# An attention and two MLPs on one core: v read in runs of 2048 bytes into 72 partitions, P summed over 8 steps

## The chip, the cores and the metric

The program runs on one core of a Trainium2 chip. The metric is the device time of one execution in microseconds. A core has TensorE (PE, with its weight loads as PEld), VectorE (DVE), ScalarE (ACT), GpSimd (POOL), SyncE (SP, which here only issues DMAs), and 16 DMA engines that move the data between main memory and the 128 partitions of the on-chip buffer.

## The reference

```python
def _attn_ref(q, k, v, p):                  # q, k, v: (8, 8, 576, 64); p: (8, 8, 32, 64)
    scale = 1.0 / np.sqrt(q.shape[-1])
    def sm_attn(qq, kk, vv):
        s = scale * np.matmul(qq, kk.transpose(0, 1, 3, 2))
        s = s - np.max(s, axis=-1, keepdims=True)
        a = np.exp(s)
        a = a / (np.sum(a, axis=-1, keepdims=True) + 1e-09)
        return np.matmul(a, vv)
    p_packed = sm_attn(p, k, v)             # 32 packed rows for each head
    return sm_attn(q, p_packed, p_packed)

x = attention, as (4608, 512)
x = (silu(x @ w_gate) * (x @ w_val)) @ w_out          # d_ff 1536
out = (((x @ w1) * (x @ w2)) @ w3) @ w_out2           # d_ff 1024
```

q, k, v and p are 32-bit floats; the weights come as 64-bit floats, which the kernel reads as integers and converts itself.

## The kernel before, in words

The program has a first stage, the packed attention, and then the two MLPs, which are almost all matrix products. The change touches the first stage alone, where `p_packed` is made.

The first stage goes over 16 units u, each of 4 heads of one batch element (`b, Q = divmod(u, 2)`). For each unit, `load_kv(u, "k")` brings a tile `km` of k, 128 partitions of 18 tokens (4608 bytes in one run), and `load_kv(u, "v")` a tile `vm` of v; both are 576 KB. In `vm` a head's 576 tokens are cut into `PK` = 96 runs of `NV` = 6 tokens: partition p has, for each of 4 heads, tokens 6p to 6p+5, one run of 1536 bytes. Then:

- `pa_kT` turns k and p by products with an identity (`pk`, `pkr`) and copies them to `kT`. p lies in the tile `zp`, for all batch elements, each row twice, the second copy made on POOL by `twice_p`.
- `pa_s` forms the scores of 32 packed rows against 576 tokens for 4 heads (`psp`) and their maximum; `pa_exp` writes the exponentials to `ap`, sorted so that the tokens of one step r (token 6p+r for all p) stand together.
- `pa_T` turns `ap` step by step (`pat`, 6 transposes of 96 columns) and ScalarE copies the result to `apT`.
- `pa_P` sums over 6 steps r and 4 heads: 24 products `pP` of `apT` with `vm`, each over 96 partitions. `pa_PT` turns the result into the tile `PTd`, which all later work uses.

The order is written out by hand: a loop over steps s issues `pa_kT(s)`, `pa_s(s-1)`, `pa_PT(s-4)`, `pa_T(s-2)`, `pa_exp(s-1)`, `pa_P(s-3)`, and every engine runs its instructions in that order. Other work is hung on steps by tables: the first q tiles (`q_rows`, 4 tiles of 576 KB) and what follows from them, `raw_load` for the first weights (512 KB each: `raw_w` in rows of 1024 bytes, `raw_wo` in rows of 4096 bytes, 128 partitions), and their conversion. All loads of the stage are issued by SP, one after the other; a load whose buffer isn't free yet holds up those behind it. There are 4 buffers for k (`KVB`) and 4 for v (`VB`):

```python
            if s < U:
                pa_kT(s)
            load_kv(s - VD, "v")
            load_kv(s + KVB, "k")
```

Two loads of later stages are used in the prediction. `raw_wo` of the second MLP is read by four loads of 32 partitions each, in rows of 4096 bytes (line 329); `x2r` is read into 128 partitions in runs of 1536 bytes (line 795).

Of the kernel before, what the change touches and what calls it, by code (L numbers as in the profile page):

```python
# [8 lines left out]
F32 = mybir.dt.float32  # L9
# [6 lines left out]
ET = mybir.EngineType  # L16
M0 = None
KVB = 4
VB = 4
VD = 0  # L20
RAW0 = (7, 8, 10, 11, 12, 13, 15, 15, 15, 16.75)
WS = {10.0: (0, 0), 11.0: (0, 1), 13.25: (1, 0), 14.25: (1, 1), 15.25: (2, 0), 16.25: (2, 1)}
# [18 lines left out]
def packed_attention_moe_kernel(  # L41
# [24 lines left out]
    nc = tc.nc  # L66
    B, H, S, D = q.shape
# [3 lines left out]
    DF2 = w1.shape[1]  # L71
    HS = S // 2
    NR = S // 32
    NV = 6
    PK = S // NV
    NF = DFF // 128
    NB32 = S // 32
# [7 lines left out]
    def pool(name, side, bufs=1, **kw):  # L85
        return tc.alloc_tile_pool(name=name, bufs=bufs, side=side, reuse_waits="tile", **kw)
# [21 lines left out]
    ident = const.tile([128, 128], F32, name="ident")  # L108
# [15 lines left out]
    def psum(name):  # L124
        ps_n[0] += 1
        return ps_at[ps_n[0] % len(ps_at)].tile([128, 2, 512], F32, tag="A", name=name)

    def psum1(name):
        return psB.tile([128, 512], F32, tag="B", name=name)
# [4 lines left out]
    hs = [slice(32 * hq, 32 * hq + 32) for hq in range(4)]  # L134

    in_front, conv_rest, pin, pin_at = [True], [], {}, {}
# [338 lines left out]
    pa = pool("pa", "left", bufs=2)  # L475

    kv = {}
    zp = pa.tile([128, B, 2, 2, 64], F32, tag="zp", name="zp", bufs=1)

    def load_p(b0, b1):  # L480
        nc.sync.dma_start(zp[:, b0:b1, :, 0], p[b0:b1].rearrange("b (q h) j d -> (h j) b q d", q=2))

    def twice_p(b0, b1):
        nc.gpsimd.tensor_copy(zp[:, b0:b1, :, 1], zp[:, b0:b1, :, 0])

    def load_kv(u, nm):
        if not 0 <= u < 2 * B:
            return
        b, Q = divmod(u, 2)
        src = {"k": k, "v": v}[nm]  # L490
        if nm == "k":
            m = pa.tile([128, NR, D], F32, tag="km", name=f"km{u}", bufs=KVB)
            nc.sync.dma_start(m, src[b, 4 * Q:4 * Q + 4].rearrange("h (p r) d -> (h p) r d", r=NR))
        else:
            m = pa.tile([PK, 4, NV, D], F32, tag="vm", name=f"vm{u}", bufs=VB)
            pin_at["sp"] = nc.sync.dma_start(m, src[b, 4 * Q:4 * Q + 4].rearrange("h (p r) d -> p h r d", r=NV))
        kv[nm, u] = m
# [3 lines left out]
    def pa_kT(u):  # L501
        km = kv.pop(("k", u))

        kT = pa.tile([128, NR // 2 + 1, 128], F32, tag="kT", name=f"kT{u}")
        b, Q = divmod(u, 2)
        t1 = psum1(f"pkr{u}")
        nc.tensor.transpose(t1[:, 128:256], zp[:, b, Q].rearrange("p e d -> p (e d)"), ident)
        t = psum(f"pk{u}")
        for m in range(NR // 2):
            nc.tensor.transpose(  # L510
                t[:, m // 4, 128 * (m % 4):128 * (m % 4) + 128] if m < 8 else t1[:, 0:128],
                km[:, 2 * m:2 * m + 2, :].rearrange("p r d -> p (r d)"), ident)
        nc.scalar.copy(kT[:, 0:8], t.rearrange("p a (m n) -> p (a m) n", n=128))
        nc.scalar.copy(kT[:, 8:10], t1[:, 0:256].rearrange("p (m n) -> p m n", n=128))
        kT_t[u] = kT

    def pa_s(u):


        kT = kT_t.pop(u)  # L520
        t = psum(f"psp{u}")
        for hq in range(4):
            for e in range(2):
                es = slice(64 * e, 64 * e + 64)
                nc.tensor.matmul(
                    t[hs[hq], e, 0:HS].rearrange("j (m p g) -> j g m p", m=3, g=3), lhsT=kT[es, 9, hs[hq]],
                    rhs=kT[es, 0:9, hs[hq]].rearrange("d (g m) p -> d g m p", g=3), start=True, stop=True, tile_position=(64 * e, 32 * hq))
        mx = pa.tile([128, 1], F32, tag="mx", name=f"mx{u}")
        nc.vector.reduce_max(mx, t[:, :, 0:HS], axis=AX.XY)
        nc.vector.tensor_scalar_mul(mx, mx, -scale)  # L530
        return t, mx

    def pa_exp(u, t, mx):
        a = pa.tile([128, NV, PK], F32, tag="ap", name=f"ap{u}")
        sm = pa.tile([128, 1], F32, tag="sm", name=f"sm{u}", bufs=3)
        nc.scalar.activation(
            a.rearrange("j (m e) p -> j e m p", e=2),
            t[:, :, 0:HS].rearrange("j e (m p) -> j e m p", p=PK),
            AF.Exp, bias=mx, scale=scale, accum_out=sm)
        ap_t[u], sm_t[u] = a, sm  # L540

    def pa_T(u):
        a, sm = ap_t.pop(u), sm_t[u]
        nc.vector.tensor_scalar(sm, sm, 1e-9, None, op0=ALU.add)
        nc.vector.reciprocal(sm, sm)
        t = psum(f"pat{u}")
        for r in range(NV):
            nc.tensor.transpose(
                t[:PK, r % 2, 128 * (r // 2):128 * (r // 2) + 128],
                a[:, r], ident)  # L550
        aT = pa.tile([PK, 2, 3, 128], F32, tag="apT", name=f"apT{u}")
        pin_at["act"] = nc.scalar.copy(aT, t[:PK, :, 0:384].rearrange("p e (m n) -> p e m n", m=3))
        apT_t[u] = aT

    def pa_P(u):
        vm = kv.pop(("v", u))
        aT = apT_t.pop(u)
        sm = sm_t.pop(u)
        t = psum1(f"pP{u}")
        for r in range(NV):  # L560
            for hq in range(4):
                nc.tensor.matmul(
                    t[hs[hq], 0:64], lhsT=aT[:, r % 2, r // 2, hs[hq]], rhs=vm[:, hq, r, :],
                    start=(r == 0), stop=(r == NV - 1), tile_position=(0, 32 * hq))
        Pd = pa.tile([128, 2, 64], F32, tag="Pd", name=f"Pd{u}")
        pin_at["dve"] = nc.vector.tensor_scalar(
            Pd, t[:, 0:64].rearrange("p (o d) -> p o d", o=1).to_broadcast([128, 2, 64]), sm, None, op0=ALU.mult)
        Pd_t[u] = Pd

    def pa_PT(u):  # L570
        t = psum1(f"pPT{u}")[:, 0:128]
        nc.tensor.transpose(t, Pd_t.pop(u).rearrange("p a b -> p (a b)"), ident)
        nc.scalar.copy(PTd[:, u], t)

    U = 2 * B
    load_p(0, 1)
    load_kv(0, "k")
    load_kv(1, "k")
    load_p(1, 3)
    load_kv(2, "k")  # L580
    load_p(3, B)
    twice_p(0, 1)
    twice_p(1, 3)
    twice_p(3, B)
    for u in range(3, KVB):
        load_kv(u, "k")
    extra = {}
# [22 lines left out]
    def run(s, slot):  # L610
        for at in [at for at in extra if s + slot <= at < s + slot + 0.25]:
            for fn, args in extra.pop(at):
                fn(*args)

    last = int(max(max(extra), U + 3))
    with tc.manual_schedule(engines=M0):
        for s in range(last + 1):
            if s < U:
                pa_kT(s)
            load_kv(s - VD, "v")  # L620
            load_kv(s + KVB, "k")
            run(s, 0)
            run(s, 0.25)
            if 0 <= s - 1 < U:
                x = pa_s(s - 1)
            if 0 <= s - 4 < U:
                pa_PT(s - 4)
            run(s, 0.5)
            if 0 <= s - 2 < U:
                pa_T(s - 2)  # L630
            if 0 <= s - 1 < U:
                pa_exp(s - 1, *x)
            if 0 <= s - 3 < U:
                pa_P(s - 3)
            run(s, 0.75)
# [466 lines left out]
```

## Time and profile before

| what | value |
|---|---|
| median of 3 runs | 1412.79 us (1408.39 to 1418.39) |
| the profiled execution | 1416.25 us |
| its span, first to last instruction | 1414.5 us |
| mean granted TensorE clock over the span | 0.987 |
| PE busy, weight loads | 1358.2 us (96%), 1246.9 us (88%) |
| DVE, ACT, POOL busy | 715.7, 576.7, 401.1 us (51%, 41%, 28%) |
| bytes moved | 230.28 MB in 182471 packets, mean 163 GB/s |

Shares of busy time are means over the whole span. The stages have different limits, so the views by stretch of time say more than this table. A busy PE is not a PE at its peak, since products are pipelined.

### The profile page before, as it was taken

What the parts mean: (1) busy time and instruction counts of PE and PEld (TensorE: products, weight loads), DVE (VectorE), ACT (ScalarE), POOL (GpSimd) and SP (SyncE); (2) the same over time, 40 slices, a digit from 0 to 9 for tenths busy, and PEclk for the clock granted to TensorE, in tenths of its full rate; (3) what the DMA queues carried; (4) which work ended last, traced back from release to release, by engine and by line L of the source; (5) the groups of instructions that cost most, each with busy time, mean ns of one, the idle gap of its engine ahead of it and who ended that gap; (6) DMA issues with size and microseconds to landing.
All of it is one profiled execution on the core that took longest, in us unless ns stands there. A gap on an engine that the chain in (4) does not pass through costs nothing.

```text
span 1414.5 us, 25679 instructions
## 1 busy us (share of the span) xinstructions
PE 1358.2 (96%) x10228; PEld 1246.9 (88%) x10228; DVE 715.7 (51%) x1016; ACT 576.7 (41%) x946; POOL 401.1 (28%) x315
## 2 busy tenths in 40 slices
PE   7778989999999999999999989999999999999998
PEld 5556988999999999998988889989989899898997
DVE  2457779636585566664255467933323423334130
ACT  4576534425243353353453334623323333333231
POOL 0234233422333323254253323702202122021120
PEclk9899999999999999999999999999999999999999
DMA  9997676544345545235443236955728448175451
GB/s 257 244 217 197 185 222 210 150 152 99 116 125 169 171 101 136 61 116 153 139 132 96 67 96 243 334 192 182 235 76 253 156 154 258 58 247 178 132 159 45
DMA packets 182471, 230.28 MB, mean 163 GB/s; under 512 B 70480, under 2 KB 113488, under 8 KB 182352
## 3 DMA queue, kind: packets, MB, share of 16 engines
q1 hardware_dynamic: 182352, 228.64, 54.9%
q8 instruction: 81, 1.33, 0.4%
q14 instruction: 38, 0.31, 0.1%
HBM read 179.04 MB, written 49.55 MB: 162 GB/s over the span
## 4 chain that ended last, share of the span: by engine, by line
PE 79%; DMA 8%; DVE 5%; issue 3%; ACT 2%; POOL 1%; SPq 1%; DVEq 0%; ACTq 0%; POOLq 0%
PE px L666 19%; PE pA L975 14%; PE po L1039 14%; PE pg L454 8%; PE pv L454 8%; PE pB L975 7%; PE pC L975 4%; PE pc L422 2%; PE pw L730 2%; DMA km<-in_k_dram 1%; DMA raw_w<-in_moe_w_gate_dram 1%; DMA vm<-in_v_dram 1%; DMA raw_w<-in_moe_w_val_dram 1%; DMA raw_wo<-in_moe_w_out_dram 1%; DVE vx_w L357 1%
## 5 line engine op out<-in xcount | busy, mean ns | idle before, releaser
L90 POOL TENSOR_TENSOR ul<-u,uh 128x576 fp32r<-128x576 f32 x96 | 153.8, 1603 | 342.3 <-ACT uh L94 330.8
L995 POOL TENSOR_TENSOR c<-s,s 128x384 f32<-128x384 f32 x48 | 49.3, 1026 | 375.5 <-ACT s L990 375.4
L666 PE MATMUL px<-uh,woh 128*128 128x384 f32 x576 | 148.0, 337 | 3.0 <-DVE acc L676 2.0
L666 PE MATMUL px<-ul,woh 128*128 128x384 f32 x576 | 147.6, 336 | 2.6 <-POOL ul L90 2.6
L666 PE MATMUL px<-uh,wol 128*128 128x384 f32 x576 | 147.3, 336 | 0.0
L990 ACT COPY s<-pA 128x384 f32<-128x384 f32 x144 | 69.2, 481 | 182.9 <-PE pA L975 180.4
L463 DVE TENSOR_TENSOR u<-u,pv 128x576 f32<-128x576 f32 x96 | 71.7, 748 | 96.4 <-PE pv L454 88.9
L94 ACT CAST uh<-u 128x576 fp32r<-128x576 f32 x96 | 64.7, 674 | 134.3 <-DVE u L463 134.3
L1039 PE MATMUL po<-wo_hi,abl 128*128 128x512 f32 x288 | 112.2, 390 | 0.0
L1039 PE MATMUL po<-wo_lo,abh 128*128 128x512 f32 x288 | 112.2, 389 | 0.0
L1039 PE MATMUL po<-wo_hi,abh 128*128 128x512 f32 x288 | 112.1, 389 | 0.0
L666 PEld LDWEIGHTS px<-uh,woh 128*128 128x128 f32 x576 | 103.7, 189 | 5.7 <-DVE acc L676 2.6
L676 DVE TENSOR_TENSOR acc<-acc,px 128x768 f32<-128x768 f32 x72 | 68.1, 948 | 78.5 <-PE px L666 78.1
L666 PEld LDWEIGHTS px<-ul,woh 128*128 128x128 f32 x576 | 104.8, 189 | 3.1 <-POOL ul L90 3.1
L666 PEld LDWEIGHTS px<-uh,wol 128*128 128x128 f32 x576 | 104.9, 189 | 0.0
L90 DVE TENSOR_TENSOR abl<-ab,abh 128x768 fp32r<-128x768 f32 x48 | 48.1, 1003 | 105.4 <-ACT abh L94 105.3
L90 POOL TENSOR_TENSOR wol<-wof,woh 128x512 fp32r<-128x512 f32 x48 | 63.8, 1341 | 99.3 <-ACT woh L94 81.3
L454 PE MATMUL pg<-aTh,ch 128*128 128x288 f32 x384 | 87.9, 311 | 2.6 <-ACT u L459 2.2
L454 PE MATMUL pv<-aTh,ch 128*128 128x288 f32 x384 | 83.7, 300 | 3.4 <-ACT u L459 3.1
L459 ACT ACTIVATE u<-pg 128x576 f32<-128x576 f32 x96 | 62.4, 650 | 52.9 <-PE pg L454 51.7
L454 PE MATMUL pg<-aTh,cl 128*128 128x288 f32 x384 | 83.4, 299 | 0.0
L454 PE MATMUL pg<-aTl,ch 128*128 128x288 f32 x384 | 83.1, 298 | 0.0
(312 smaller groups left out, 3192.0 us busy)
## 6 DMA issues: line engine op xcount, KB each, us to landing
ws<-wsd SPq DMA_DIRECT2D x245, 256.0 KB, 3.1
wf<-Wd SPq DMA_DIRECT2D x36, 512.0 KB, 4.5
wsd<-ws SPq DMA_DIRECT2D x49, 256.0 KB, 3.0
km<-in_k_dram SPq DMA_DIRECT2D x16, 576.0 KB, 18.5
vm<-in_v_dram SPq DMA_DIRECT2D x16, 576.0 KB, 19.4
wof<-wod SPq DMA_DIRECT2D x36, 256.0 KB, 3.1
x2r<-X2d SPq DMA_DIRECT2D x24, 384.0 KB, 4.9
out_dram<-o SPq DMA_DIRECT2D x36, 256.0 KB, 2.0
```

The lines of the kernel that those rows point to most:

```text
L90: return eng.tensor_tensor(out=out, in0=src, in1=hi.bitcast(F32), op=ALU.subtract)
L94: nc.scalar.copy(hi, src)
L422: nc.tensor.matmul(t[hs[at], b, Q], lhsT=PTd[es, 2 * (2 * P + b) + Q, hs[hq]], rhs=w[es, 2 * Q + hq // 2].rearrange("p g n -> p (g n)"), s ...
L454: nc.tensor.matmul(t[:, hf, 0:HS], lhsT=w[:, b % 2, Q, cols], rhs=x[:, Q, hf, :], start=first, stop=last,)
L459: x = nc.scalar.activation(u, t[:, :, 0:HS], AF.Silu)
L463: x = nc.vector.tensor_tensor(out=u, in0=u, in1=t[:, :, 0:HS], op=ALU.mult)
L666: nc.tensor.matmul(t[:, h, 0:CW], lhsT=w[:, 128 * d:128 * d + 128], rhs=x[:, CW * c:CW * c + CW], start=first, stop=last,)
L676: nc.vector.tensor_tensor(out=o, in0=o, in1=t[:, :, 0:CW], op=ALU.add)
L975: nc.tensor.matmul(bk[n], lhsT=w[:, hl, 128 * d:128 * d + 128], rhs=r[:, d], start=(first and d == 0 and i == 0), stop=(d == 1 and i == 2) ...
L990: nc.scalar.copy(o, t)
L995: on.tensor_tensor(out=r, in0=o, in1=t, op=op)
L1039: nc.tensor.matmul(t, lhsT=a[:, j, cols], rhs=w[:, f], start=first, stop=last)
```

## The change

A head's tokens are cut into 72 runs of 8 tokens (`NV = 8`, `PK = 72`): one run is 2048 bytes, and `vm` fills 72 partitions with 8192 bytes each (before 96 with 6144). There are three v tiles, not four; the three take as much room as the four did. P is turned in 8 transposes of 72 columns and summed over 8 steps of 72 rows, 32 products. The scores are written in another order, tokens as (p m) with 9 pairs m next to each other, and the exponential reads them with a stride of 4 and writes `ap` sorted by step. The tile `zp` keeps p once, and each unit's doubled copy is made one step ahead in a small tile `z2`. In SP's order the k load of a step now stands ahead of its v load.

```diff
-VB = 4
+VB = 3
-    NV = 6
+    NV = 8
     PK = S // NV
-    zp = pa.tile([128, B, 2, 2, 64], F32, tag="zp", name="zp", bufs=1)
+    zp = pa.tile([128, B, 2, 64], F32, tag="zp", name="zp", bufs=1)
+    z2_t = {}
...
-    def twice_p(b0, b1):
-        nc.gpsimd.tensor_copy(zp[:, b0:b1, :, 1], zp[:, b0:b1, :, 0])
+    def twice_p(u):
+        b, Q = divmod(u, 2)
+        z2_t[u] = pa.tile([128, 2, 64], F32, tag="z2", name=f"z2{u}")
+        nc.gpsimd.tensor_copy(z2_t[u], zp[:, b, Q:Q + 1].to_broadcast([128, 2, 64]))
...
-        nc.tensor.transpose(t1[:, 128:256], zp[:, b, Q].rearrange("p e d -> p (e d)"), ident)
+        nc.tensor.transpose(t1[:, 128:256], z2_t.pop(u).rearrange("p e d -> p (e d)"), ident)
...
-                    t[hs[hq], e, 0:HS].rearrange("j (m p g) -> j g m p", m=3, g=3), lhsT=kT[es, 9, hs[hq]],
-                    rhs=kT[es, 0:9, hs[hq]].rearrange("d (g m) p -> d g m p", g=3), start=True, stop=True, tile_position=(64 * e, 32 * hq))
+                    t[hs[hq], e, 0:HS].rearrange("j (p m) -> j m p", m=9), lhsT=kT[es, 9, hs[hq]],
+                    rhs=kT[es, 0:9, hs[hq]], start=True, stop=True, tile_position=(64 * e, 32 * hq))
...
-            t[:, :, 0:HS].rearrange("j e (m p) -> j e m p", p=PK),
+            t[:, :, 0:HS].rearrange("j e (p m) -> j e m p", p=PK),
...
-        aT = pa.tile([PK, 2, 3, 128], F32, tag="apT", name=f"apT{u}")
-        pin_at["act"] = nc.scalar.copy(aT, t[:PK, :, 0:384].rearrange("p e (m n) -> p e m n", m=3))
+        aT = pa.tile([PK, 2, NV // 2, 128], F32, tag="apT", name=f"apT{u}")
+        pin_at["act"] = nc.scalar.copy(aT, t[:PK].rearrange("p e (m n) -> p e m n", n=128))
...
-    twice_p(0, 1)
-    twice_p(1, 3)
-    twice_p(3, B)
+    twice_p(0)
...
-            load_kv(s - VD, "v")
             load_kv(s + KVB, "k")
+            load_kv(s, "v")
+            if s + 1 < U:
+                twice_p(s + 1)
```

On SP, the loads behind the first four k tiles stand so before (`vm0` is unit 0's v tile, `km4` unit 4's k tile, `qr0_0` a q tile; the number behind the last underscore only numbers tiles; then partitions and elements):

```order
L496 DMA vm0_137<-in_v_dram 96x4x384
L493 DMA km4_139<-in_k_dram 128x1152
L166 DMA qr0_0_141<-in_q_dram 128x1152
L496 DMA vm1_158<-in_v_dram 96x4x384
L493 DMA km5_160<-in_k_dram 128x1152
L166 DMA qr0_1_162<-in_q_dram 128x1152
L496 DMA vm2_194<-in_v_dram 96x4x384
```

and so with the change:

```order
L496 DMA km4_136<-in_k_dram 128x1152
L499 DMA vm0_138<-in_v_dram 72x4x512
L166 DMA qr0_0_142<-in_q_dram 128x1152
L496 DMA km5_159<-in_k_dram 128x1152
L499 DMA vm1_161<-in_v_dram 72x4x512
L166 DMA qr0_1_165<-in_q_dram 128x1152
L496 DMA km6_197<-in_k_dram 128x1152
```

The k and v loads of a step have changed places, with the step's q load still behind both, and a v load names 72 partitions with 4 runs of 512 elements where it named 96 with 4 runs of 384.

On PE, one step before, from the scores of unit 3 to the k of unit 5:

```order
L525 MATMUL psp3_329<-kT3_224 32x3x96 x8
L572 MATMUL pPT0_341<-ident_66,Pd0_294 128x128
L548 MATMUL pat2_346<-ident_66,ap2_266 96x128 x6
L562 MATMUL pP1_358<-vm1_158,apT1_264 32x64 x24
L507 MATMUL pkr5_386<-ident_66,zp_105 128x128
L510 MATMUL pk5_388<-ident_66,km5_160 128x128 x8
```

and the same step with the change:

```order
L528 MATMUL psp3_350<-kT3_231 32x9x32 x8
L575 MATMUL pPT0_362<-ident_66,Pd0_313 128x128
L551 MATMUL pat2_367<-ident_66,ap2_277 72x128 x8
L565 MATMUL pP1_381<-vm1_161,apT1_275 32x64 x32
L510 MATMUL pkr5_417<-ident_66,z25_334 128x128
L513 MATMUL pk5_419<-ident_66,km5_159 128x128 x8
```

The order of the step is the same; `pat` has 8 instructions for 6, `pP` 32 for 24, and the turned p comes from the unit's own `z2` tile.

## Rows read from the trace of the kernel before

**Rows 1.** The page, the span in 40 slices of 35.4 us, tenths busy.

```profile
PE   7778989999999999999999989999999999999998
...
DMA  9997676544345545235443236955728448175451
GB/s 257 244 217 197 185 222 210 150 152 99 116 125 169 171 101 136 61 116 153 139 132 96 67 96 243 334 192 182 235 76 253 156 154 258 58 247 178 132 159 45
DMA packets 182471, 230.28 MB, mean 163 GB/s; under 512 B 70480, under 2 KB 113488, under 8 KB 182352
```

**Rows 2.** Busy time by stage (us of the span; instructions in brackets).

```profile
core 0: us, PE busy (x) PEld busy (x) DVE busy (x) ACT busy (x) POOL busy (x), PEclk, DMA share, GB/s
0.00:112.00 112.00, 80.74 (x1386) 58.88 (x1386) 49.60 (x126) 66.75 (x120) 25.94 (x27) 0.92 1.06 245
112.00:118.00 6.00, 5.05 (x120) 4.45 (x119) 2.45 (x9) 5.25 (x8) 1.30 (x1) 1.00 0.67 178
138.00:1414.50 1276.50, 1254.33 (x8544) 1168.65 (x8544) 647.53 (x859) 494.47 (x802) 362.36 (x281) 0.99 0.51 156
```

**Rows 3.** The chain of waits up to 118 us: start, length, what.

```profile
9.86 16.74 DMA km<-in_k_dram
26.66 19.71 DMA vm<-in_v_dram
46.39 20.18 DMA raw_w<-in_moe_w_gate_dram
...
68.02 1.51 PE pP L562 x48
...
73.16 0.66 PE pat L548 x6
73.81 0.85 PE pP L562 x48
...
76.53 17.86 DMA raw_w<-in_moe_w_val_dram
...
104.72 10.37 DMA raw_wo<-in_moe_w_out_dram
```

**Rows 4.** The DMA view of 4 to 112 us; KB and median us to landing.

```profile
DMA packets 15649, 26.96 MB, mean 250 GB/s; under 512 B 2557, under 2 KB 12869, under 8 KB 15636
...
q1 hardware_dynamic: 15636, 26.77, 107.4%
...
vm<-in_v_dram SPq DMA_DIRECT2D x16, 576.0 KB, 19.4
km<-in_k_dram SPq DMA_DIRECT2D x13, 576.0 KB, 18.8
```

**Rows 5.** Five stretches by what was being loaded, columns as in rows 2.

```profile
4.50:7.50 3.00, 2.24 (x11) 2.24 (x12) 0.00 (x0) 0.23 (x1) 0.14 (x1) 1.00 1.05 360
28.00:40.00 12.00, 10.37 (x202) 7.48 (x201) 6.98 (x18) 6.77 (x13) 1.32 (x2) 0.89 1.07 230
108.50:111.50 3.00, 1.21 (x47) 0.92 (x36) 1.74 (x5) 2.32 (x4) 1.43 (x2) 1.00 1.05 394
529.30:531.30 2.00, 2.00 (x38) 1.64 (x41) 0.71 (x2) 1.49 (x3) 0.73 (x1) 1.00 1.02 261
1016.00:1019.60 3.60, 3.60 (x17) 2.97 (x16) 0.72 (x1) 0.84 (x1) 0.00 (x0) 1.00 0.97 325
```

**Rows 6.** Packets by length in three of these stretches: 28:40, 529.3:531.3, 1016:1019.6.

```profile
DMA packets 1306, 2.76 MB, mean 230 GB/s; under 512 B 79, under 2 KB 1025, under 8 KB 1305
...
DMA packets 451, 0.52 MB, mean 261 GB/s; under 512 B 48, under 2 KB 363, under 8 KB 451
...
DMA packets 783, 1.17 MB, mean 325 GB/s; under 512 B 49, under 2 KB 709, under 8 KB 782
```

**Rows 7.** What SP's queue waited for up to 118 us: total, times, longest.

```profile
SPq L496 <- DMA vm<-in_v_dram: 5.9, 3, 2.9
...
SPq L496 <- PE pP L562: 4.3, 3, 2.8
SPq L493 <- DMA km<-in_k_dram: 4.3, 3, 2.0
...
SPq L496 <- DMA km<-in_k_dram: 3.9, 3, 2.3
...
SPq L493 <- DMA vm<-in_v_dram: 3.4, 2, 2.7
```

**Rows 8.** Groups up to 118 us: busy us, mean ns, idle before; last, one POOL copy.

```profile
L513 ACT COPY kT<-pk 128x1024 f32<-128x1024 f32 x16 | 16.2, 1010 | 18.6 <-PE pk L510 18.5
L552 ACT COPY apT<-pat 96x768 f32<-96x768 f32 x16 | 12.9, 804 | 4.0 <-PE pat L548 4.0
L525 PE MATMUL psp<-kT 64*32 64x288 f32 x256 | 12.3, 433 | 0.4 <-ACT apT L552 0.4
L536 ACT ACTIVATE ap<-psp,mx 128x576 f32<-128x576 f32 x16 | 11.8, 740 | 2.4 <-DVE sm L544 1.4 <-PE pk L510 1.0
L90 POOL TENSOR_TENSOR aTl<-aT,aTh 128x576 fp32r<-128x576 f32 x4 | 7.0, 1738 | 34.5 <-ACT aTh L94 34.5
L347 ACT ACTIVATE wf<-raw_w 128x512 f32<-128x512 f32 x8 | 5.3, 676 | 12.2 <-DMA raw_w<-in_moe_w_gate_dram 9.3 <-DMA raw_w<-in_moe_w_val_dram 2.9
L190 PE MATMUL psq<-qT,PTd 64*32 64x288 f32 x64 | 2.9, 415 | 0.0
...
2.77 0.29 POOL L484 COPY zp<-zp 128x128 f32<-128x128 f32 x1 [1.47 <-DMA zp<-in_p_dram]
```

More of the change, by code (lines that the diff above doesn't have):

```diff
@@ L477, in packed_attention_moe_kernel @@
     kv = {}
-    zp = pa.tile([128, B, 2, 2, 64], F32, tag="zp", name="zp", bufs=1)
+    zp = pa.tile([128, B, 2, 64], F32, tag="zp", name="zp", bufs=1)
+    z2_t = {}
     def load_p(b0, b1):
-        nc.sync.dma_start(zp[:, b0:b1, :, 0], p[b0:b1].rearrange("b (q h) j d -> (h j) b q d", q=2))
-    def twice_p(b0, b1):
-        nc.gpsimd.tensor_copy(zp[:, b0:b1, :, 1], zp[:, b0:b1, :, 0])
+        nc.sync.dma_start(zp[:, b0:b1], p[b0:b1].rearrange("b (q h) j d -> (h j) b q d", q=2))
+    def twice_p(u):
+        b, Q = divmod(u, 2)
+        z2_t[u] = pa.tile([128, 2, 64], F32, tag="z2", name=f"z2{u}")
+        nc.gpsimd.tensor_copy(z2_t[u], zp[:, b, Q:Q + 1].to_broadcast([128, 2, 64]))
     def load_kv(u, nm):
```

## The prediction

> **What bounds the kernel now.** I read the slices of the page first. TensorE is busy nine tenths or more almost everywhere, but not in the first three slices (7, 7, 8), and these are also the ones in which the DMA engines stand at nine tenths and most bytes move [rows 1]. By stage: from 0 to 112 us PE is busy 80.74 of 112 us while the mean DMA share is 1.06 (over 1, since packets overlap on an engine); from 138 us to the end PE is busy 1254 of 1276 us [rows 2]. All of the change lies in the first stage, so it is worth what that stage gains or loses. The chain of waits up to 118 us is a row of landings: 16.74 us for a k tile, 19.71 for a v tile, 20.18, 17.86 and 10.37 for raw weights, 85 of 118 us, with a few microseconds of TensorE between them [rows 3]. So the first stage ends when its bytes are in. Between 4 and 112 us 26.96 MB went through at 250 GB/s, in a queue that was never empty (107.4%); a k or v tile of 576 KB takes about 19 us from issue to landing [rows 4], which at 250 GB/s is 4.7 MB, eight transfers in flight. What comes behind the last landing is TensorE-bound and moves with it; I count a microsecond of the transfer time as a microsecond of the kernel.
>
> **What a v tile costs today.** Not all bytes cost the same [rows 5]. With k tiles alone in flight (4.5 to 7.5 us) the rate is 360 GB/s, so a k tile costs 1.64 us. With k, q and v tiles mixed (28 to 40 us) it is 230 GB/s at the same share. The packets of that stretch [rows 6]: 1306 less 1025 are the 4608-byte packets of k and q, 281 or 2.19 tiles; 1025 less 79 are the 1536-byte packets of v, 946 or 2.46 tiles. At 1.64 us the k and q tiles take 3.60 of the 12 us, so a v tile takes 8.40/2.46 = 3.41 us, twice a k tile for the same bytes. The whole stage says the same: 17.5 MB that are not v at 360 to 394 GB/s take 44.4 to 48.6 us, which leaves 59.4 to 63.6 us for 16 v tiles, 3.7 to 4.0 us each.
>
> Is it the length of the packets or the place where they land? A later load of 1536-byte packets, into 128 partitions, runs at 325 GB/s at share 0.97; the weights with rows of 1024 bytes, with 4096-byte ones, at 394 at 1.05. Four loads that land in 32 partitions each, in packets of 4096 bytes (88 packets, 0.36 of the 0.52 MB of that stretch), fall to 261 at 1.02 [rows 5, 6]. So short packets into 128 partitions are fast and long ones into few partitions slow: the slow thing about v is its 96 partitions, not its 1536 bytes. [...]
>
> **The change, part by part.**
>
> The v loads. A tile is the same 576 KB, now 72 partitions times 4 heads times 2048 bytes: 288 packets, not 384. The partition counts 128, 96 and 32 of all loads of this stage divide by 16, so 16 engines can have equal shares of whole partitions; the v load now has 6 partitions, 24 packets, on each. 72 does not: 4.5 partitions each. If shares must be equal, the largest number of engines up to 16 that divides 72 is 12, with 6 partitions and 24 packets each as now, of 2048 bytes. No row shows a count of this kind, so it is an assumption that I take. [...]
> With 12 engines each of them has 4/3 of the v bytes. Low end: only the bytes at the pace of a k tile count, 1.64/3 = 0.55 us a tile, 16 tiles, +8.7 us. High end: all of what a v tile costs grows by a third, 3.41/3 to 4.0/3, +18.2 to +21.2 us. The 72 partitions are still nearer to the 32-partition load than the 96 were, and that one is stretched; so I don't take the low end but the middle of the whole, **+15 us**. A gain from fewer packets is the third rival.
>
> Three v tiles, k ahead of v in SP's queue. The buffer of v of unit s is now free when the products pP of unit s-3 are done, at the end of step s, not s-4. So SP stands in front of the v load for most of a step, and the step's q or raw load and the next k load stand behind it. v gets three steps of lead instead of nearly four: a step is 118/19 = 6.2 us, so 18.6 us against 19.4 to landing [rows 2, 4]. But landing takes 19 us because eight transfers are queued; one issued later stands behind fewer. SP waits on earlier landings already (5.9 + 4.3 + 3.9 + 3.4 us) as much as on TensorE's pP (4.3) [rows 7], and the engines stay full. Cost 0 as long as some transfers are queued; with 4 k and 2 to 3 v tiles out there are. If not: fifth case below.
>
> TensorE. The pP products go from 24 to 32 a unit (48 to 64 records). Back to back 48 took 0.85 us, at the lower clock 1.51 [rows 3], so +0.28 to +0.50 us. The transposes of P go from 6 to 8; 6 took 0.66, so +0.22. Over 16 units +8 to +11.5 us, in a stage in which PE has 31 us idle [rows 2]; covered by the landings, but for the last unit, where some +0.6 us lie behind the last v tile. The scores are the same 8 products with another stride at the output; the q scores, written without a gap, take 415 ns and these 433 [rows 8], so 0.
>
> ScalarE. The copy apT grows from 768 to 1024 columns: 0.80 us to about 1.01, as the kT copy of 1024 [rows 8], +0.21 a unit, 3.4 us in all; the exp reads PSUM with a stride of 4 in place of none, bounded by the weights' strided pass, 676 ns for 512 columns against 740 for the 576 here, at most +0.1 us a unit; ACT is idle 45 of 112 us [rows 2]. Covered.
>
> POOL. Three copies of p become 16 of 128x128 at 0.29 us [rows 8], 4.6 us in place of 1.4, one step ahead of their use; POOL works 26 of 112 us, its longest instruction in the stage 1.74 us [rows 8] against a step of 6.2. Covered.
>
> Sum: +15 us, the tail within rounding. Against the profiled execution, 1416.25 us, that is 1431; it lies 3.5 us above the median of the runs, so against the median of 1412.79: **1428 us**.
>
> **The rivals.**
> 1. 72 partitions do go over all 16 engines, in fours and fives, or the stretch of v is a limit common to all engines that doesn't care how many work. Then a tile costs what it does: 5 partitions on the fullest engine, 20 packets of 2048 bytes against 24 of 1536, +11% of 1.64 us, 16 tiles, +2.9 us at most: 1413 to 1416. [...] Against: the 32-partition row says that narrow loads get worse.
> 2. The equal shares are 9 or 8 partitions on 8 or 9 engines: a tile's bytes an engine grow by 16/9 or 16/8 in place of 4/3. At the low end's scale that is +1.28 or +1.64 us a tile, +20 or +26 us, 1433 or 1439; only a count of engines below 12 gets there.
> 3. The other side, faster: a v tile's price is one per packet. Its place is each engine's queue between 8 and 104 us, its price 3.4 to 4.0 us per 384 packets, and it decides if the price per packet stays as the packets get longer: 288 packets are a quarter less, 0.85 to 1.0 us a tile, -14 to -16 us, 1398. Against it the 1536-byte load into 128 partitions, above.
> 4. The change doesn't do what it says, runs of 2048 bytes being cut again: then the count of packets shows it, and the time is rival 1's.
> 5. With three tiles SP does run dry: v comes 0.8 us late in 13 steps, +10 us beside whatever the engines do. With twelve engines some 1438, with sixteen 1425.
>
> **How the numbers follow.** Forecast (12 engines): 0.66, rival 1 with 4: 0.19, rival 2: 0.03, rival 3: 0.07, rival 5: 0.05. One per cent, 14.1 us, is about what a measurement of this kernel can tell from no change. The forecast's own range, +8.7 to +21.2, lies across that line: I give it 0.40 above and 0.26 below. Slower by over 1%: 0.40 + 0.03 + 0.05 = 0.48. Within: 0.26 + 0.19 = 0.45. Faster: 0.07. Range: the forecast's reach, 1421.5 to 1434, and down past rival 1 to 1411, as the runs of before scatter by 4 to 6 us around their median; left out are rivals 2, 3 and part of 5, some 0.15.
>
> **What will show it.** The page's count of packets falls by 1536 if the runs are 2048 bytes. In 28 to 40 us each tile leaves 79/4.65 = 17 packets under 512 bytes, about one for each engine it used; with 12 engines for v those under 512 bytes fall by 16 x 4 = 64, with 16 not at all. In the stage's windows the DMA share should fall below 1 (four engines idle on v) and the rate to some 220 GB/s, and the last raw_wo land near 130 us, not 115. If the share stays at 1.07 and the stage ends near 115 us, rival 1; if it ends near 100, rival 3. If the share falls and PE's waits name pP from SP, rival 5. The stages behind should keep their lengths; a change there would make the prediction wrong in a way that it doesn't foresee.

## The result, and the profile after

The changed kernel takes 1426.51 us (median of 8 runs) against 1411.72 for the kernel before on the same chip: +14.8 us between the medians. The ratio taken over the runs is 1.009, 95% interval 1.0067 to 1.0113, which is 12.7 us, between 9.5 and 16.0. The profiled execution took 1426.35 us, its span is 1424.6. One run of the kernel with the work of 8 steps, below, took 6605 us and is left out of its median and ratio.

In the two profiled executions, 10.1 us apart, all of the difference lies in the first stage. The first product with `w_out` (`px`, the second half of the first MLP) begins at 142.8 us in the kernel before and at 153.3 in the changed one; from there to the end of the span it is 1271.7 and 1271.3 us. Single executions scatter, the kernel before between 1402 and 1421 us over all its runs in this document, and its profiled one is 4.5 us above its median; so a few microseconds between two profiles show nothing by themselves. The view of tile `px`, first the kernel before, then the changed one (durations in ns, then first and last start in us):

```profile
L666 PE MATMUL px<-uh,woh x576: 332/334/522, 142.8 to 862.2; 128*128 128x384 f32 x192
```

```profile
L669 PE MATMUL px<-uh,woh x576: 331/334/522, 153.3 to 872.4; 128*128 128x384 f32 x192
```

The page of the changed kernel, slices and packets, answers to [rows 1]:

```profile
PE   7779989999999999999999999999999999999998
...
DMA  9986565752455544326334226955728548275451
...
DMA packets 180873, 230.31 MB, mean 162 GB/s; under 512 B 70416, under 2 KB 107280, under 8 KB 180752
```

The same bytes go in 1598 fewer packets. Those under 512 bytes fall from 70480 to 70416, by 64, four for each of 16 v loads: if every engine that a load uses leaves one short packet, as the count in [rows 6] suggests, each v load used twelve engines where it had used sixteen. Of the remaining 1534, the runs of 2048 bytes in place of 1536 account for 1536 (two packets of instruction loading came in beside them, 83 for 81). By stretch, columns as in [rows 2]:

```profile
28.00:100.00 72.00, 54.45 (x1026) 38.79 (x1022) 31.79 (x84) 37.76 (x67) 17.02 (x20) 0.86 0.91 214
100.00:112.00 12.00, 9.35 (x177) 7.17 (x166) 6.75 (x16) 9.74 (x16) 3.51 (x3) 0.86 0.43 100
```

The kernel before, in the same two stretches:

```profile
28.00:100.00 72.00, 53.80 (x965) 38.97 (x963) 36.05 (x93) 42.52 (x78) 18.16 (x14) 0.89 1.08 232
100.00:112.00 12.00, 8.30 (x176) 5.96 (x176) 7.19 (x16) 11.05 (x20) 5.65 (x4) 1.00 1.09 274
```

Up to 100 us the DMA share is 0.91 for 1.08 and the rate 214 for 232 GB/s; then, from 100 to 112 us, the engines are more than half idle. The chain of waits of the changed kernel, answering to [rows 3], shows what stood there: a weight tile that took 21 us to land, behind a v load, and ScalarE and TensorE behind it in their order.

```profile
57.88 20.33 DMA raw_w<-in_moe_w_val_dram
...
80.99 21.21 DMA raw_w<-in_moe_w_val_dram
102.26 0.56 issue
...
104.02 0.68 ACT sg_w L354
104.70 0.91 ACT apT L555
```

No load stands on this chain after 102.2 us; in the kernel before one ended there at 115.1 [rows 3]. SP itself stood from 100.89 to 111.59 us in front of the last two v loads:

```profile
100.89 10.70 SPq L499 DMA_DIRECT2D vm<-in_v_dram  x2
```

The longest of its waits there is 6.2 us for a product `pP`, that is, for one of the three v buffers. The first `raw_wo` load behind them was issued at 113.5 us where it had been 101.3.

SP's queue up to 135 us, answering to [rows 7] (total us, times, longest), waits in front of v loads (L499) for 48 us in three rows:

```profile
SPq L499 <- DMA vm<-in_v_dram: 20.1, 9, 3.8
SPq L499 <- PE pP L565: 19.2, 5, 6.2
SPq L331 <- DVE wf L360: 9.8, 2, 9.7
SPq L499 <- PE pkr L510: 8.9, 4, 3.2
```

And the groups up to 126 us, answering to [rows 8]: the copy `apT` went from 804 to 1018 ns, the exponential kept its 742 with a stride of 4, the scores went from 433 to 499, and a copy of p on POOL takes 291. The longer scores are not the new order's: their median is 427 ns for 403, and in the kernel with 6 steps and the same new order (`after_six_steps`, below) it is 404. The granted clock from 28 to 100 us is 0.86 for 0.89.

```profile
L555 ACT COPY apT<-pat 72x1024 f32<-72x1024 f32 x16 | 16.3, 1018 | 5.6 <-PE pat L551 5.5
...
L528 PE MATMUL psp<-kT 64*32 64x288 f32 x256 | 14.3, 499 | 0.0
L539 ACT ACTIVATE ap<-psp,mx 128x576 f32<-128x576 f32 x16 | 11.9, 742 | 2.1 <-PE pk L513 1.2 <-DVE sm L547 1.0
```

### The profile page after: what moved, and what is told of

It is laid out like the page before. It is cut to its first block, busy times and chain, and to the rows that moved or that the text cites. A ratio compares the mean times of both kernels' runs of the same rounds, so it can differ in the third digit from the quotient of the medians.

```text
span 1424.6 us, 26277 instructions
## 1 busy us (share of the span) xinstructions
PE 1370.9 (96%) x10516; PEld 1254.4 (88%) x10516; DVE 716.6 (50%) x1016; ACT 579.8 (41%) x946; POOL 403.2 (28%) x328
## 2 busy tenths in 40 slices
DMA packets 180873, 230.31 MB, mean 162 GB/s; under 512 B 70416, under 2 KB 107280, under 8 KB 180752
## 4 chain that ended last, share of the span: by engine, by line
PE 81%; DMA 7%; DVE 5%; issue 3%; ACT 2%; POOL 1%; SPq 0%; DVEq 0%; ACTq 0%; POOLq 0%
PE px L669 19%; PE pA L978 14%; PE po L1042 14%; PE pg L454 9%; PE pv L454 8%; PE pB L978 7%; PE pC L978 4%; DMA raw_w<-in_moe_w_val_dram 3%; PE pc L422 3%; DMA vm<-in_v_dram 2%; PE pw L733 2%; DVE vx_w L357 1%; PE psq L207 1%; DMA raw_w<-in_moe_w_dram 1%; PE pk L513 1%
## 5 line engine op out<-in xcount | busy, mean ns | idle before, releaser
L90 POOL TENSOR_TENSOR ul<-u,uh 128x576 fp32r<-128x576 f32 x96 | 153.3, 1597 | 337.1 <-ACT uh L94 320.3
L454 PEld LDWEIGHTS pg<-aTh,ch 128*128 128x128 f32 x384 | 62.2, 190 | 24.2 <-issue 9.0
```

The lines of the kernel that those rows point to most:

```text
L90: return eng.tensor_tensor(out=out, in0=src, in1=hi.bitcast(F32), op=ALU.subtract)
L454: nc.tensor.matmul(t[:, hf, 0:HS], lhsT=w[:, b % 2, Q, cols], rhs=x[:, Q, hf, :], start=first, stop=last,)
```

## The experiments

Theory A is the prediction's: twelve engines carry what sixteen did. Theory B: the third v buffer's loss makes SP wait and the engines run dry. Theory C: the work that the change adds or reorders on TensorE, ScalarE and POOL is paid after all. Each ratio is against the kernel before on the same chip, with its 95% interval, and is not the quotient of the two medians beside it.

### One part of the change alone

Three buffers, and nothing else:

```diff
-VB = 4
+VB = 3
```

> The kernel before with three v buffers, not four, and nothing else changed (96 partitions, 6 steps, v ahead of k in SP's queue). If twelve engines made the change slow (theory A), three buffers cost nothing by themselves: within 3 us of before, the DMA share of 4 to 112 us stays above 1.0. If the third buffer made SP wait and the DMA engines run dry (theory B), most of the 15 us is here: +8 us or more, with stretches of a share below 0.5 towards the end of the stage. If both act only together, this run shows +0 to +4 and the split of v below decides.

Measured: 1410.65 against 1413.71 us, 0.9976 (0.9956 to 0.9995). Three buffers cost nothing by themselves; theory B alone is out. That SP stands still is no loss in itself: here it waits 40.8 us for `pP` in front of v loads, twice the 19.2 of the changed kernel.

```profile
SPq L496 <- PE pP L562: 40.8, 13, 6.0
SPq L496 <- DMA vm<-in_v_dram: 13.7, 6, 4.2
```

The rest of the change without the new cut, with four buffers:

```diff
-VB = 3
+VB = 4
-    NV = 8
+    NV = 6
...
-        pin_at["act"] = nc.scalar.copy(aT, t[:PK].rearrange("p e (m n) -> p e m n", n=128))
+        pin_at["act"] = nc.scalar.copy(aT, t[:PK, :, 0:64 * NV].rearrange("p e (m n) -> p e m n", n=128))
```

> The changed kernel with v cut back to 96 partitions of 6 tokens, 6 steps and four v buffers; the order k ahead of v, the doubled p unit by unit on POOL and the scores' new order stay. Theory A and theory B both say: back at before, within 3 us. If the reordering or the POOL copies cost something themselves (theory C), it stays slower by 5 us or more.

Measured: 1409.99 against 1413.71 us, 0.9974 (0.9954 to 0.9994). The order in SP's queue, the copies on POOL and the new order of the scores cost nothing together. The price is in the cut into 72 partitions and 8 steps, by itself or together with the three buffers. (No run has the changed kernel with four buffers.)

The work of 8 steps without the loads of 8:

```diff
-VB = 4
+VB = 3
...
+        for r in range(2):
+            nc.tensor.transpose(t[:PK, r, 384:512], a[:, r], ident)
+        aT = pa.tile([PK, 2, 4, 128], F32, tag="apT", name=f"apT{u}")
+        pin_at["act"] = nc.scalar.copy(aT, t[:PK].rearrange("p e (m n) -> p e m n", n=128))
...
+        for r in range(2):
+            for hq in range(4):
+                nc.tensor.matmul(
+                    t[hs[hq], 64:128], lhsT=aT[:, r % 2, r // 2, hs[hq]], rhs=vm[:, hq, r, :],
+                    start=(r == 0), stop=(r == 1), tile_position=(0, 32 * hq))
```

> The kernel before with three v buffers (by themselves 0.24% faster than before) and the work of 8 steps on TensorE and ScalarE beside the loads of 6: two more transposes, eight more products into an unused part of the same bank, and a copy of 1024 columns for 768 in each unit. The result is not touched, the extra work is thrown away. Theory L says that this work is covered by the loads: within 4 us of before. If TensorE's or ScalarE's extra work is what the change pays (theory C), +8 to +15 us.

Measured: 1413.73 against 1412.16 us, 1.0028 (1.0008 to 1.0049). Against the kernel before that is 4 us, as theory L (below) said. But the kernel with three buffers alone stood at 0.9976, so the work itself costs about 0.5%, 7 us. That is a difference of two ratios taken on two chips, and by their intervals it may be 3 to 11 us: theory C has a part of the price.

### v on sixteen engines

The v tile of the changed kernel in two loads, of 64 and of 8 partitions:

```diff
-            pin_at["sp"] = nc.sync.dma_start(m, src[b, 4 * Q:4 * Q + 4].rearrange("h (p r) d -> p h r d", r=NV))
+            rows = src[b, 4 * Q:4 * Q + 4].rearrange("h (p r) d -> p h r d", r=NV)
+            for p0, p1 in ((0, 64), (64, 72)):
+                pin_at["sp"] = nc.sync.dma_start(m[p0:p1], rows[p0:p1])
```

> The changed kernel with each v tile read by two loads, partitions 0 to 63 and 64 to 71: the same 72 partitions, packets of 2048 bytes, 8 steps and three buffers, but 64 divides by 16, so all 16 engines carry v. Theory A: 10 to 15 of the 15 us come back, 1411 to 1417, and packets under 512 bytes rise to 70480 + 16 x 8 = 70608. Theory B: nothing comes back, 1424 to 1428, since the buffers are the same. If the stretch comes from few partitions alone, whatever the count of engines: about +5 to +15 us stay.

Measured: 1432.79 against 1413.71 us, 1.0133 (1.0104 to 1.0163). Nothing comes back. The engines did change: the share from 28 to 100 us is 1.06 again, where the changed kernel has 0.91, and the rate is 202 GB/s, no higher than its 214. (The packets under 512 bytes, 70608, are as expected for 16 + 8, but 12 + 12 gives the same.) Theory A in its plain form fell here.

```profile
28.00:100.00 72.00, 54.15 (x1061) 39.05 (x1050) 30.02 (x78) 34.06 (x61) 17.31 (x21) 0.88 1.06 202
```

Its control, the same in two loads of 36 partitions (measured alone below, a pair with k has a share of 0.92 this way and 1.04 as 64 + 8):

```diff
-            for p0, p1 in ((0, 64), (64, 72)):
+            for p0, p1 in ((0, 36), (36, 72)):
```

> The changed kernel with each v tile read by two loads of 36 partitions; 36 is divided by 12 as 72 is, so 12 engines carry v, three partitions each and load. The control of the run with 64 + 8, which had 16 engines on the same 72 partitions, also in two loads, and ended 1.3% above before. If the split itself costs time (more loads for the same bytes in flight), this run is as slow as that one, 1430 to 1436, and the count of engines decides nothing. If the split is free and sixteen engines really are no better than twelve, this one stands at the changed kernel's 1424 to 1430. Theory A (twelve engines are the price) needs this run slower than the one with 64 + 8, above 1436.

Measured: 1423.54 against 1410.09 us, 1.0107 (1.007 to 1.0145): no worse than the changed kernel's one load, and if anything better than sixteen engines, though the intervals overlap. Two loads in place of one aren't what kept the run with 64 + 8 slow. Which partitions share a load differs too, though, and that matters below (64 + 32 against 32 to 95 with 0 to 31), so this pair doesn't say what sixteen engines would be worth at a better place. It also has three buffers and no gap at the end: its profile shows a share of 0.88 and 236 GB/s from 100 to 112 us, where the changed kernel has 0.43 and 100; `px` still begins at 149.1 us, 6.3 later than in the kernel before. So, as far as one profile of each tells, the gap isn't the whole price; how much of it is stays open.

### Loads alone

Two kernels that only load, one layout behind the other, all on SP's queue into eight buffers; a small store marks the end of each stretch. The output isn't computed.

```python
        for u in range(16):
            for kind in kinds:
                one[kind](u)(t8[n % 8])     # one v or k tile in this layout
                n += 1
        for i, t in enumerate(t8):
            nc.vector.tensor_copy(mark[:, i:i + 1], t[:, 0:1])
        nc.sync.dma_start(out[0:128, :], mark)
```

> Loads alone, no attention and no MLP, the output is not computed: eleven stretches of 16 tiles of 576 KB each (the last three of 16 pairs), one layout after the other. In order: k in 128 partitions of 4608 bytes; the same bytes in 128 partitions of 3 x 1536; v in 96 partitions by one load; v in 72 by one load; 72 as 64 + 8; 96 as 72 + 24; 96 as 64 + 32; v in 64 partitions of 9 tokens; then pairs of k with v in 96, in 72, in 64 + 8. Theory A: k 350 to 400 GB/s; 3 x 1536 nearly as fast, 320 or more; v in 96 170 to 240; v in 72 by one load at a share of about 0.75 and a rate a quarter below that of 96, 130 to 180; 64 + 8 above that by a fifth or more; 96 as 72 + 24 (twelve engines) well below 96 as 64 + 32 (sixteen). The rival, a limit common to all engines: v in 72 as fast as or faster than v in 96, and no difference between 72 + 24 and 64 + 32. The rival of a price per packet: 3 x 1536 as slow as v in 96, and 72 faster than 96 by a quarter.

> Loads alone, no attention and no MLP, the output is not computed: eleven stretches of 16 tiles (the last six of 16 pairs). In order: v in partitions 0 to 95; v in 16 to 111; v in 0 to 71; in 28 to 99; 64 partitions of 9 tokens in 32 to 95; then pairs of k with v in 16 to 111, in 28 to 99, in 0 to 71 as 36 + 36, in 0 to 95 as 72 + 24, in 0 to 95 as 64 + 32; last, pairs of k with k read in runs of 1536 bytes. A tile took 2.3 us in 0 to 95 and 3.3 us in 0 to 71 before. Theory L, that the place decides, namely how evenly the partitions below 64 and from 64 up share the bytes: 16 to 111 (half and half) near a k tile's 1.6 us, 28 to 99 below 2.3 us although it has the same 12 engines and the same packets as 0 to 71, 32 to 95 near 1.7. Theory A, that the count of engines decides: 28 to 99 as slow as 0 to 71, 3.2 us or more, and 16 to 111 as 0 to 95. The pairs the same way: 36 + 36 against 5.8 us (0 to 71) and 5.9 (64 + 8) tells whether the split costs; 72 + 24 (12 engines) against 64 + 32 (16 engines) tells what the engines are worth on the same partitions.

The view by stretch of the first, each cut out of the middle of a layout (only DVE, POOL, the clock, DMA share and GB/s have columns). In order: k in 128 partitions; the same bytes in runs of 1536; v in 96; in 72; 72 as 64 + 8; 96 as 72 + 24; 96 as 64 + 32; 64 partitions, 0 to 63; then pairs of k with 96, with 72, with 64 + 8.

```profile
3.00:24.00 21.00, 0.92 (x6) 0.00 (x0) 1.00 1.02 412
28.00:40.00 12.00, 0.00 (x0) 0.00 (x0) 1.00 1.06 376
56.00:84.00 28.00, 0.77 (x5) 0.00 (x0) 1.00 1.09 257
95.00:136.00 41.00, 0.81 (x6) 0.00 (x0) 1.00 0.82 188
148.00:186.00 38.00, 0.77 (x5) 0.00 (x0) 1.00 1.03 202
200.00:236.00 36.00, 0.77 (x5) 0.00 (x0) 1.00 0.84 201
248.00:278.00 30.00, 0.77 (x5) 0.00 (x0) 1.00 1.10 236
289.00:305.00 16.00, 0.00 (x0) 0.00 (x0) 1.00 1.05 213
335.00:400.00 65.00, 0.77 (x5) 0.00 (x0) 1.00 1.07 246
415.00:490.00 75.00, 0.62 (x4) 0.00 (x0) 1.00 0.90 207
510.00:585.00 75.00, 0.46 (x3) 0.00 (x0) 1.00 1.04 198
```

The same view of the second, by place: v in partitions 16 to 111; 0 to 71; 28 to 99; 64 partitions, 32 to 95; then pairs of k with v in 16 to 111, in 28 to 99, in 0 to 71 as 36 + 36, in 72 + 24 and in 64 + 32 (both 0 to 95); last, pairs of k tiles, one of the two in runs of 1536 bytes. The stretch of v in 0 to 95, measured again here, gave 246 GB/s, so the same layout differs by 4% between the two runs (257).

```profile
50.00:78.00 28.00, 0.77 (x5) 0.00 (x0) 1.00 1.09 265
88.00:126.00 38.00, 0.92 (x6) 0.00 (x0) 1.00 0.80 196
136.00:170.00 34.00, 0.92 (x6) 0.00 (x0) 1.00 0.81 238
180.00:198.00 18.00, 0.61 (x4) 0.00 (x0) 1.00 1.05 394
215.00:275.00 60.00, 0.77 (x5) 0.00 (x0) 1.00 1.06 249
290.00:355.00 65.00, 0.61 (x4) 0.00 (x0) 1.00 0.91 229
375.00:437.00 62.00, 0.61 (x4) 0.00 (x0) 1.00 0.92 235
455.00:530.00 75.00, 0.68 (x5) 0.00 (x0) 1.00 0.92 207
550.00:605.00 55.00, 0.38 (x3) 0.00 (x0) 1.00 1.07 259
620.00:660.00 40.00, 0.61 (x4) 0.00 (x0) 1.00 1.04 392
```

What is to be read there:

- Not the length of the runs. 1536 bytes into 128 partitions go at 376 GB/s; 96 partitions with runs of the same length at 257, and a pair of k tiles of which one is cut that way at 392.
- Twelve engines: v in 72 partitions runs at a share of 0.80 to 0.82 where k in 128 has 1.02 and v in 96, in one load or as 64 + 32, 1.09 to 1.10.
- The place. 64 partitions are as fast as 128 when they are 32 to 95 (394 GB/s) and half as fast when they are 0 to 63 (213), with the same packets and the same share, 1.05. 72 partitions run at 238 in 28 to 99 and at 196 in 0 to 71, at shares of 0.81 and 0.80. How the place does this was not shown. A limit of 213 GB/s that the 64 lower partitions share doesn't give the sizes: if they took their bytes at that rate and the others went beside them, 0 to 71 would reach 240 GB/s by this estimate and 0 to 95 would reach 320, where 188 to 202 and 201 to 257 were measured. Nor does the even share below and above 64 that theory L supposed: moving 96 partitions to 16 to 111, half on each side, does little (265 for 246 to 257, 2.23 us a tile where 1.6 was expected), so an even share of the tile as a whole is not enough.
- The count of engines at the same place: 72 on twelve 188 to 196, as 64 + 8 on sixteen 202 (share 1.03); 96 as 72 + 24 201 (0.84), as 64 + 32 236 (1.10). Sixteen engines buy little on partitions 0 to 71, and a sixth on 0 to 95; in pairs with k a quarter (207 and 259, shares 0.92 and 1.07).
- A pair of k and v, 1.18 MB, takes 4.80 us at 246 GB/s with v in 96 and 5.70 at 207 with v in 72: +0.90 us, times 16, +14.4 us. As 64 + 8 it is no better (198). Either pair takes 1.1 us more than a k tile and a v tile measured apart (1.43 + 2.30 and 1.43 + 3.14 us); why isn't shown.

The view of the packets in the stretches of v in 96 (54 to 88 us) and of v in 72 (92 to 140 us):

```profile
DMA packets 5892, 8.70 MB, mean 256 GB/s; under 512 B 240, under 2 KB 5862, under 8 KB 5892
```

```profile
DMA packets 4636, 9.11 MB, mean 190 GB/s; under 512 B 190, under 2 KB 190, under 8 KB 4635
```

That is 14.8 tiles with 16.3 packets under 512 bytes each, and 15.4 tiles with 12.3. One for each engine is sixteen and twelve; the 64 missing short packets of the changed kernel and the share of 0.82, three quarters of 1.09, agree.

### The place and the count, in the kernel before

Theory L, from the first of these: the price of v is where it lands. In the kernel before, with all its arithmetic, v's 96 partitions in two loads in three ways:

```diff
+VP = ((0, 72), (72, 96))      # or ((0, 64), (64, 96)), or ((32, 96), (0, 32))
...
-            pin_at["sp"] = nc.sync.dma_start(m, src[b, 4 * Q:4 * Q + 4].rearrange("h (p r) d -> p h r d", r=NV))
+            rows = src[b, 4 * Q:4 * Q + 4].rearrange("h (p r) d -> p h r d", r=NV)
+            for p0, p1 in VP:
+                pin_at["sp"] = nc.sync.dma_start(m[p0:p1], rows[p0:p1])
```

> The kernel before, only each v tile read by two loads, partitions 0 to 71 and 72 to 95: both counts are divided by 12, so twelve engines carry v, to the same 96 partitions in the same packets of 1536 bytes; steps, buffers, order and arithmetic are those of before. In the loads measured alone, a pair of k and v took 5.92 us this way against 4.86 by one load: times 16, +17 us. If what a pair of loads takes is what the kernel pays (theory L and A both), this kernel stands at +12 to +20 us. If the stage is bound by something else (TensorE, ScalarE, the buffers: theory C), it stays within 4 us of before.

> The control: the kernel before with each v tile read by two loads, partitions 0 to 63 and 64 to 95, both divided by 16: sixteen engines, the same 96 partitions, two loads as well. Alone a pair of k and v took 4.71 us this way against 4.86: -2 us, so within 4 us of before. If the splitting in two itself costs time in the kernel, as half the bytes per load are in flight, this one is slower by 5 us or more, and the run with 72 + 24 has to be read against this one.

> The kernel before with each v tile read by two loads, partitions 32 to 95 first and 0 to 31 behind it. 64 partitions from 32 to 95 (half of them below 64, half above) took 1.72 us a tile alone where 0 to 63 took 2.8, so I expect the pair of k and v below 4.7 us, and the kernel faster than before by 3 to 10 us, if splitting costs nothing. If splitting costs, it stands where the run with 64 + 32 does; theory C says no difference.

Measured against 1412.16 us: 72 + 24, 1424.68, 1.0095 (1.006 to 1.013); 64 + 32, 1421.26, 1.0067 (1.004 to 1.0093); 32 to 95 and then 0 to 31, 1407.84, 0.9973 (0.9955 to 0.9991). The last two have the same engines (shares of 1.08 and 1.06 from 28 to 100 us), the same packets, the same partitions and two loads each; only which partitions share a load differs, and they are 13 us apart. So 72 + 24 came out in the range expected, 64 + 32 outside it. Twelve engines against sixteen are 3 us apart with overlapping intervals, and from 28 to 100 us they move 231 and 226 GB/s, at shares of 0.95 and 1.08. That 64 + 32 costs 9 us in the kernel is not explained: alone its pair with k is no slower than one load's (259 for 246 GB/s). Weight loads between them or half-sized loads in the queue may do it; no run parts these. What the place does was measured in the kernel for 96 partitions only; the changed kernel with v in partitions 28 to 99 wasn't run.

The profile of the kernel with 32 to 95 first also shows what comes next when loads are fast. From 28 to 100 us it moves 279 GB/s, then the loads are nearly over. (The 232 of the kernel before is not the place alone: with three buffers and the same loads to the same partitions the profiled execution has 259.)

```profile
28.00:100.00 72.00, 59.10 (x1149) 42.41 (x1150) 45.69 (x109) 52.62 (x96) 23.87 (x18) 0.93 1.06 279
100.00:112.00 12.00, 10.97 (x144) 9.59 (x143) 8.60 (x18) 6.39 (x11) 2.72 (x2) 1.00 0.25 71
```

Its last `pP` is at 103.2 us, 13.4 earlier than before, but `px` begins at 135.5, only 7.3 earlier: in these two executions half is given back, in a stretch where SP's weight loads wait for VectorE's conversions (the longest 10.2 us).

```profile
SPq L332 <- DVE wf L361: 12.9, 2, 10.2
SPq L148 <- DVE qT L159: 9.5, 1, 9.5
```

### Two versions meant to be faster

v as k is read, in 128 partitions, with P turned by VectorE in 32x32 blocks and 18 steps of 32 rows:

```diff
-            m = pa.tile([PK, 4, NV, D], F32, tag="vm", name=f"vm{u}", bufs=VB)
-            pin_at["sp"] = nc.sync.dma_start(m, src[b, 4 * Q:4 * Q + 4].rearrange("h (p r) d -> p h r d", r=NV))
+            m = pa.tile([128, NV, D], F32, tag="vm", name=f"vm{u}", bufs=VB)
+            pin_at["sp"] = nc.sync.dma_start(m, src[b, 4 * Q:4 * Q + 4].rearrange("h (p r) d -> (h p) r d", r=NV))
...
+        aT = pa.tile([128, NV, 32], F32, tag="apT", name=f"apT{u}")
+        pin_at["dve"] = nc.vector.transpose(out=aT.rearrange("p r j -> p (r j)"), in_=a.rearrange("p r j -> p (r j)"))
...
-                    t[hs[hq], 0:64], lhsT=aT[:, r % 2, r // 2, hs[hq]], rhs=vm[:, hq, r, :],
-                    start=(r == 0), stop=(r == NV - 1), tile_position=(0, 32 * hq))
+                    t[hs[hq], 0:64], lhsT=aT[hs[hq], r, :], rhs=vm[hs[hq], r, :],
+                    start=(r == 0), stop=(r == NV - 1), tile_position=(32 * hq, 32 * hq))
```

> v read as k is: 128 partitions with 18 tokens each, one run of 4608 bytes; P turned by one 32x32 block transpose on VectorE in place of 8 on TensorE and a copy on ScalarE, and summed over 18 steps of 32 rows for each head, 72 products a unit; four v buffers, the rest as in the changed kernel. Theory L (the price of v is that it lands in part of the partitions) says that a v tile then costs what a k tile does, 1.6 us in place of 3.4 to 4.0: the DMA-bound stage would shrink by 29 to 38 us, and TensorE, busy 81 of 112 us and given some 1.5 us more a unit, is the bound before that: 10 to 25 us faster than before. A price per packet or per run says some 10 us or more as well, so this run doesn't part those two. Theory A says nothing against it. If the first stage were not bound by its loads at all, it comes out at before or slower.

Measured: 1428.02 against 1410.09 us, 1.0124 (1.0091 to 1.0158): slower by 18 us where 10 to 25 faster were expected. The loads did get out of the way, the share from 28 to 100 us is 0.61 and SP waits for TensorE (54.3 us for `pkr`, 15.6 for `pP`, up to 130 us); but the 72 products a unit (144 records) hold PE 42.2 us and leave it idle 21.9 us between them, 18.7 of them in "issue", time in which it waited for nothing that the profile shows.

```profile
28.00:100.00 72.00, 56.66 (x1813) 43.93 (x1805) 39.22 (x94) 31.31 (x62) 17.50 (x21) 0.91 0.61 204
```

```profile
L560 PE MATMUL pP<-vm,apT 32*32 32x64 f32 x2304 | 42.2, 227 | 21.9 <-issue 18.7 <-ACT kT L517 2.0 <-ACT PTd L571 0.7
```

```profile
L562 PE MATMUL pP<-vm,apT 96*32 96x64 f32 x768 | 15.5, 227 | 11.5 <-issue 5.4 <-ACT PTd L573 4.6 <-ACT kT L514 1.2
```

The last line is the kernel before's. I had reckoned 1.5 us a unit more for these products; 64.1 us for 16 units in place of 27.0 are 2.3 more. The 0.8 us over are 13 us in all, of the 28 or more by which the expectation missed; what the others are stays open.

The three parts that gained, together: the changed kernel's order and POOL copies with `NV = 6`, `VB = 3` and the loads 32 to 95, 0 to 31.

> What gained, taken together: the changed kernel's order (k ahead of v, p doubled unit by unit) with v cut into 96 partitions and 6 steps, three v buffers, and each v tile read by two loads, partitions 32 to 95 and then 0 to 31. The three parts alone stood at 0.9974, 0.9976 and 0.9973 of before. If each helps in its own way, 0.990 to 0.995, 1398 to 1405 us; if they all remove the same wait, 0.996 to 0.999, about 1408. Slower than before would say that the gains of the single parts were scatter.

Measured: 1407.76 against 1413.18 us, 0.9965 (0.9945 to 0.9986). It beats both kernels, by little. That fits the second case, parts that remove the same wait, better than the first; which wait that is was not shown, and the interval just reaches the first.

## Why the prediction held, point by point

1. "The first stage ends when its bytes are in", and what lies behind keeps its length: the second half is right, 1271.7 and 1271.3 us from `px` on. The first half is right only in part. In the changed kernel the last landing on the chain of waits is at 102.2 us; behind it the chain is computing, while SP stands in front of the last two v loads until 111.59. And it is wrong for a gain: a microsecond of load time was not a microsecond of the kernel when the loads got faster (half was given back with 32 to 95; all of it, and more, with v in 128).
2. Twelve engines: an assumption, and right for 72 partitions: 64 short packets fewer, 12.3 a tile in the loads alone where 96 partitions leave 16.3, and a share of 0.82 for 1.09. No row of the kernel before showed it.
3. The price of a v tile, +0.94 us taken between 0.55 and 1.33: the loads alone show +0.90 for a pair of k and v. The size was right. Its reason, a third more bytes on each of twelve engines, was not what bound it: sixteen engines on the same 72 partitions are no faster (202 against 188 to 196 GB/s, in the kernel 1.0133), while the same twelve engines on 28 to 99 are (238). That few partitions stretch a load, for which the prediction took the 32-partition row, is right only by place: 64 partitions can be as fast as 128 (394 GB/s for 376 to 412).
4. Three buffers: cost nothing alone, as forecast. In the changed kernel SP does run dry between 100 and 112 us, rival 5's sign, behind a weight tile that landed late and a v buffer that came free late. Whether a fourth buffer would have helped there stays open.
5. TensorE, ScalarE and POOL "covered": the step that was mis-sized. The durations came out as worked out (1018 ns for 1010, 291 for 290; the scores' new order costs nothing, 404 for 403), but the work of 8 steps costs about 7 us (3 to 11), not within rounding. The 1.51 us for 48 products at "the lower clock" had a granted clock of 0.50 (68.02 to 69.53 us of the kernel before), the 0.85 us one of 1.00. I take it that work in order behind a late weight tile is not hidden; the chain after 102.2 us looks so, no run shows it by itself.
6. The sum of +15 is therefore not its one term, and that it lies so near to the measured 14.8 (12.7 by the ratio) is in part luck: about 7 us of work, which the sum had at nothing, less some 3.5 that the buffers or the order gain, and the rest, 9 to 11, for the loads and for what the parts do together, where the loads alone would say 14.4. These come from different chips and need not add up to the microsecond; no run measures the rest by itself.
7. Rival 1's "limit common to all engines" was nearer to the cause than its price of 0 to 2.9 us: more engines on the same partitions 0 to 71 bought nothing in the kernel (1.0133 with 64 + 8), and the narrower place lowered the rate, from 201 to 257 GB/s in 0 to 95 to 188 to 202 in 0 to 71. Rival 3, a price per packet, is out by the 376 GB/s of 1536-byte runs in 128 partitions, and by the longer runs of v being slower (188 to 196 for 246 to 257).

## What to carry to other kernels

Before cutting a load into longer runs, look at which partitions it fills: measured alone, a load's rate here was set by its place first (213 or 394 GB/s for 64 partitions), then by the count of engines that its cut put to work (96 partitions at 201 as 72 + 24 with a share of 0.84, at 236 as 64 + 32 with 1.10), and not by the length of the runs (1536 bytes went at 376 into 128 partitions). The cut into 72 showed in the profile as 64 missing short packets and a DMA share of 0.91 where 96 partitions had 1.08 (28 to 100 us). And where loads bound a stage, price the work that hides under them too: here it cost some 7 us in a stage where TensorE was idle for 31 us of 112 and ScalarE for 45.

## What was not expected of the hardware

- 64 partitions from 32 to 95 load at 394 GB/s, 128 at 376 to 412; 64 from 0 to 63 at 213.
- 96 partitions in one load give 246 to 257 GB/s, and moving them to 16 to 111 changes that to 265 only.
- 144 records of small products a unit left TensorE 18.7 us of "issue" gaps in the stage, where 48 left 5.4 in the kernel before.
